# Four instead of six of the first expert's feature blocks in plain fp32

## The chip, the cores and the metric

The kernel runs on one core of a Trainium2 chip. The metric is device time in microseconds of one execution, as the median of several runs. The engines are named as in the profile: PE (TensorE, matmuls), PEld (TensorE's weight loads), DVE (VectorE), ACT (ScalarE), POOL (GpSimd) and SP (SyncE, which here only issues loads).

## The reference

```python
x = retention(q, k, v)                 # 8 batches, 8 heads, 576 positions, 64 wide -> 4608 tokens x 512
g_idx = argmax(x @ w_group)            # 4 groups
e_idx = argmax(x @ w_expert[g_idx])    # 4 experts in the group: 16 experts in all
h  = maximum(x[mine] @ w1[g, e], 0)    # 512 -> 1024, for the tokens of expert (g, e)
ye = h @ w2[g, e]                      # 1024 -> 512
out[mine] = (g_w * e_w)[:, None] * ye  # weights of the two softmaxes
```

Everything is fp32. A token goes through one expert of the sixteen.

## The kernel before

**Stages.** The first stage goes over 36 tiles of 128 tokens: retention, the gates, the choice of an expert, and a place for each token in a table `xs` in device memory, sorted by expert, into which an indirect store on POOL writes the weighted token row (`xnat_store`). The second stage goes over the experts, the fullest first, in steps `p` = 0 to 15, and a last pass for the rest of the first expert. Step 0 takes only the first 256 rows of the first expert and begins while the last tiles of tokens are still being routed.

**A step.** `xload(p)` loads the rows of the step's expert from `xs` into `xb` (four loads on SP). `xturn` turns them to features x tokens (`xTf`, on DVE, in three parts; for step 0 in two). Then come eight blocks `f` of 128 hidden features each: `layer1(p, f)` makes `ph` = w1 block x tokens, and ACT takes the relu of it, `hh`; `layer2(p, f)` adds w2 block x `hh` to the outputs `py`. In program order `layer2` runs one block behind `layer1`. Weights come in pieces of two blocks: piece `pc` holds blocks 2 pc and 2 pc + 1, a w1 part `r1` and a w2 part `r2` of 512 KB each.

**Split and plain.** A value is split in a high part in a shorter format (ACT, `xTh`, `wh`, `hh`) and the remainder (DVE, `xTl`, `wl`, `hl`), and a product is then three matmuls: high x high, high x low, low x high. `xsplit` splits the tokens, `wsplit` a weight part in two halves (ACT then DVE for each), and `layer1` makes `hh` and `hl` from `ph`. A plain block (`whole(p, f)`: step 0 and `f < WHOLE`) needs none of this: one fp32 matmul on `xTf` and the raw weights `r`, and a relu on ACT. The call `split(2 * pc + f % 2 + 3)` in block `f` splits a part that is used some blocks later: in step 0, block `f` splits part `(f + 3) % 2` of piece `(f + 3) // 2`.

**Order.** PE's order is the order of the program, written by hand. Instructions of DVE, ACT, POOL and SP are chained in program order too where they go through `Ordered` (their line is L117 for all of them, the line of that helper). Each engine works off its own list; waits between engines are by semaphores.

**Around the change.** In step 0 `pick(1)` finds the second expert from a count of most of the tokens. `choose`, `places` and `weigh` route the last group of three tiles (names ending in 35 for the routing, tokens in `xt_last`), `tiles_counted` and `count_experts` make the final counts `cnt` and the rows `pad1` that lie behind the second expert's last token, `xpad(1)` stores rows of zeros there, and `xload(1)` loads the second expert's rows. `rank_experts` (rows `key` to `order` on DVE) sorts the experts. Loads of `xs` wait for earlier stores to it; the stores, of different rows each, don't wait for one another (`apart`).

In block `f == WHOLE` of step 0 (`ahead`) two things differ: `layer2` of the block before comes ahead of `layer1`, and two of the three turns of step 1's rows stand between:

```python
            ahead = (p, f) == (0, WHOLE)
            if ahead:
                layer2(*prev)
                for i in range(2):
                    xturn(1, i, 3)
            layer1(p, f)
```

Of the kernel before, what the change touches and what calls it, by code (L numbers as in the profile page):

```python
# [26 lines left out]
CMAX = CAPS[0]  # L27
EARLY = 256
PICK = 26
WHOLE = 6  # L30
RB = 7
LOADS = 7
WARM = 8
# [32 lines left out]
def moe_retention(ctx, tc, qk, kv, wgt, w1, w2, c_f, out):  # L66
# [8 lines left out]
    xs = dp.tile([E * NS, Q * WQ], F32, name="xs")  # L75
# [16 lines left out]
    last = {}  # L92
# [30 lines left out]
    dve, act, pool, sp = [Ordered(e_) for e_ in (nc.vector, nc.scalar, nc.gpsimd, nc.sync)]  # L123

    def apart(key, inst):

        inst = getattr(inst, "ins", inst)
        tc.declare_no_dep(inst, group=key, reason="rows apart")
        tc.add_to_no_dep_group(key, inst)


    ereg = {}
# [25 lines left out]
    def load_piece(i, parts=(0, 1)):  # L158
        if i < len(pieces):
            raws.setdefault(i, []).extend(wload(*pieces[i], part) for part in parts)  # L160
# [5 lines left out]
    def whole(p, f):  # L166

        return p == 0 and f < WHOLE

# [10 lines left out]
    def ttiles(p):  # L180
        return [(r, min(P, CS[p] - r)) for r in range(0, CS[p], P)]

    def ring(name):

        return gp.tile([P, NB * WQ], F32, name=name, tag="ring", bufs=4)

    def nblocks(p):
        return -(-CS[p] // 32)

    def natural(p):  # L190
        return p in (0, E)
# [26 lines left out]
    def expert_of(p):  # L218
        ereg[p] = nc.values_load(
            order[0:1, p : p + 1] if p % E > 1 else eai[p % E][0:1, 0:1],  # L220
            engines=[mybir.EngineType.SP], min_val=0, max_val=E - 1,
        )

    def xload(p):

        if p >= NPASS:
            return
        if p not in ereg:
            expert_of(p)
        r0 = EARLY if p == E else 0  # L230
        nb = nblocks(p)
        mine = xs.rearrange("(e r) c -> e r c", e=E)[bass.ds(ereg[p], 1)]
        xb = ring(f"xb_{p}").rearrange("p (b w) -> p b w", w=WQ)
        for a in range(Q):
            i_ = sp.dma_start(
                xb[32 * a : 32 * a + 32, 0:nb, :],
                mine[:, r0 : r0 + 32 * nb, a * WQ : (a + 1) * WQ].rearrange("o (b t) c -> t (o b) c", t=32),
            )

            tc.add_to_no_dep_group("xs", i_.ins)  # L240
        xg[p] = xb
        if natural(p):
            nt = len(ttiles(p))
            idn = gp.tile([P, 3, 1], F32, name=f"idn_{p}", tag="idn", bufs=2)
            i_ = sp.dma_start(
                idn[:, 0:nt],
                mine[:, r0 : r0 + nt * P, DQ : DQ + 1].rearrange("o (i p) c -> p (o i) c", p=P),
            )
            tc.add_to_no_dep_group("xs", i_.ins)
            idns[p] = idn  # L250

    def xpad(p):

        apart("xs", pool.indirect_dma_start(
            out=xs, out_offset=bass.IndirectOffsetOnAxis(ap={0: pad0, 1: pad1}.get(p, pads[:, p % E : p % E + 1]), axis=0),
            in_=zero, in_offset=None, bounds_check=E * NS - 1, oob_is_err=False,
        ))
# [12 lines left out]
    def xturn(p, part, of):  # L270

        if part == 0:
            xTs[p] = xpair(f"m{p}")
            if p == 0:

                xTf[p] = wp.tile([P, NKC, EARLY], F32, name="xTf_0", tag="wl1", bufs=3)
            else:
                xTf[p] = ring(f"xTf_{p}")[:, 0 : NKC * CMAX].rearrange("p (k c) -> p k c", k=NKC)
        nb = nblocks(p)
        b0, b1 = nb * part // of, nb * (part + 1) // of  # L280
        dve.transpose(
            xTf[p][:, :, 32 * b0 : 32 * b1].rearrange("p k (b t) -> p b k t", t=32),
            xg[p][:, b0:b1, 0:DQ].rearrange("p b (k f) -> p b k f", f=32),
        )
# [64 lines left out]
    rows = {}  # L349
# [51 lines left out]
    def logits(t):  # L401

        plt = ps_sm.tile([P, RG, P], F32, name=f"plt_{t}", tag="sm")
        for i in range(NKC):
            pe.matmul(  # L405
                plt[32 * i : 32 * i + 32], wgp[:, i, :], tiles[t]["xTg"][:, i], start=True, stop=True
            )
        tiles[t]["lt"] = sm.tile([P, RG, P], F32, name=f"lt_{t}", tag="lt")
        act.copy(tiles[t]["lt"], plt)
# [661 lines left out]
    for p in range(E):  # L1071
        for f in range(NFC):
            pc = p * NPIECE + f // 2
            if p == 0:
                new = {2: (4,), 5: (7,)}.get(f, ())
            else:
                new = range(pc + 3, pc + 5) if f % 2 == 0 else ()
            for i in new:
                if i not in raws and (i >= len(pieces) or pieces[i][0] in ereg):
                    load_piece(i)  # L1080
            if (p, f) == (0, 2):
                load_piece(5, (0,))
            if (p, f) == (0, 0):
                prev = (p, f)
                continue
# [7 lines that stand above are left out]
            if (p, f) == (0, 1):  # L1093
                for t in range(NT - RG, NT):
                    xnat_rows(t)
                places_pe(NT - 4)
                places(NT - 4)
                logits(NT - 1)
                xnat(NT - 6)
                pick(1)  # L1100
                expert_of(1)
            if (p, f) == (0, 2):
                xnat(NT - 4)
                places_pe(NT - 1)
                places(NT - 1)
                weigh(NT - 1)
                xnat(NT - 3, ps_sm)
            if (p, f) == (0, 3):
                xnat(NT - 1, ps_sm)
                xload(1)  # L1110
                load_piece(5, (1,))
                load_piece(6)
            if (p, f) == (0, 4):
                for kc in range(NKC):
                    xsplit(0, kc)
            if (p, f) == (0, 6):
                xturn(1, 2, 3)
                for kc in range(NKC):
                    xsplit(1, kc)
            if 2 * pc + f % 2 + 3 >= WHOLE:  # L1120
                split(2 * pc + f % 2 + 3)
            if not ahead:
                layer2(*prev)
            if f == 0:
                for i in range(NKC if p > 1 else 2):
                    yturn(p - 1, i) if p > 1 else finish(0, i)
            if (p, f) == (0, 1):
                gate_pe(NT - 1)
                choose(NT - 1)
                xnat(NT - 5)  # L1130
            if (p, f) == (0, 2):
                tiles_counted()
                count_experts()
                xnat(NT - 2)
            if (p, f) in ((0, 4), (1, 0), (1, 1)):
                next(ranks, None)
            if (p, f) == (0, 6):
                expert_of(2)
            if f == NFC - 3 and p < E - 1:
                width_of(p + 1)  # L1140
            if (p, f) == (1, 1):
                ids(1)
            if p > 1 and f > 0:
                for b in range(2 * (f - 1), 2 * f):
                    if b < nblocks(p - 1):

                        pool.tensor_copy(pace, hts[p, f][0][0:1, 0:1].bitcast(F32))
                    ystore(p - 1, b)
            if (p, f) == (1, 2):
                xpad(2)  # L1150
                sp.dma_start(cf[:, KC_TRI:KC], c_f[:, KC_TRI:KC])
            if (p, f) == (1, 3):
                xload(2)
            if f == 4 and p and p + 2 <= E:
                xpad(p + 2)
            if f == 5 and p:
                xload(p + 2)
            if (p, f) == (2, 3):
                ov = overflow_places(cp)
                ovt = overflow_tables(*ov, mp, phs, cnt, cf, req, ident, ones, pe, dve)  # L1160
            if p in (2, 3):
                next(ovt, None) if (p, f) >= (2, 3) else None
            if f == NFC - 3 and p:
                for i in range(3):
                    xturn(p + 1, i, 3)
            if f == NFC - 2 and p:
                for kc in range(NKC):
                    xsplit(p + 1, kc)
            if f == NFC - 1 and 0 < p < E - 1:
                ids(p + 1)  # L1170
            if (p, f) in ((5, NFC - 1), (10, NFC - 1), (14, NFC - 1), (E - 1, NFC - 2)):

                pool.drain(fusable=False)
            prev = (p, f)
# [297 lines left out]
```

## Time and profile before

| | us |
|---|---|
| median of 3 runs | 589.14 (588.27 to 590.32) |
| the profiled execution | 589.66 |
| its span, first to last instruction | 587.8 |

The profile's page gives the share of the span in which each engine was busy (PE 97%, DVE 72%, ACT 55%, POOL 44%), and the share of each in the chain of work that ended last (PE 89%, DVE 3%, DMA 2%). The timeline lists instructions of an engine in order of time: start and duration in us, engine, line, operation, output<-inputs with buffer numbers left out, sizes, and in brackets the idle time of the engine before it with what ended it. A row of merged instructions has xN. Times in this document are from the start of the span. The first stage reaches to some 152 us, step 0 from 148 to 183 us, steps 1 to 15 to 566 us.

### The profile page before, as it was taken

How to read it: one execution, taken by the hardware profiler on the slowest of the kernel's cores; microseconds unless marked ns; L12 is line 12 of the kernel's file. 1: busy time of each engine (PE TensorE's matmuls, PEld its weight loads, DVE VectorE, ACT ScalarE, POOL GpSimd, SP SyncE). 2: the span in 40 equal slices, each digit the busy share in tenths (PEclk: the TensorE clock that was granted, in tenths of full speed). 3: DMA queues.
4: the chain of work that ended last, by engine and by line, in shares of the span. 5: the costliest groups of instructions: out<-in, count | busy, mean ns of one | idle time of the engine just before them, and what ended most of it. 6: DMA issues, size and time to landing. Idle time of an engine off the chain costs nothing.

```text
span 587.8 us, 16813 instructions
## 1 busy us (share of the span) xinstructions
PE 572.7 (97%) x6045; PEld 535.8 (91%) x6045; DVE 424.7 (72%) x997; ACT 325.3 (55%) x849; POOL 260.8 (44%) x391
## 2 busy tenths in 40 slices
PE   8999899999999999999999999999999999999995
PEld 6888788787769999999999999999999999999994
DVE  4877767768669677966767675867768687687784
ACT  5677787777356445444545444444545455455563
POOL 0022333224332027473636457383654836638454
PEclk9999999999999999999999999999999999999999
DMA  8999899965988961929285656839286594855841
GB/s 325 406 398 343 313 351 341 319 254 156 369 237 329 212 265 59 332 64 325 71 317 138 250 142 255 278 114 335 77 313 176 215 305 118 312 167 218 306 189 38
DMA packets 62410, 143.03 MB, mean 243 GB/s; under 512 B 9425, under 2 KB 30297, under 8 KB 62304
## 3 DMA queue, kind: packets, MB, share of 16 engines
q1 hardware_dynamic: 52944, 121.24, 59.3%
q0 software_dynamic: 9216, 20.28, 9.5%
q8 instruction: 73, 1.20, 0.8%
q14 instruction: 33, 0.27, 0.1%
q10 hardware_dynamic: 144, 0.05, 0.0%
HBM read 121.27 MB, written 24.81 MB: 249 GB/s over the span
## 4 chain that ended last, share of the span: by engine, by line
PE 89%; DVE 3%; issue 2%; DMA 2%; ACT 2%; POOL 1%; SPq 0%; POOLq 0%; ACTq 0%; DVEq 0%
PE ph L593 32%; PE py L995 11%; PE py L997 11%; PE py L996 11%; PE px L790 5%; PE pss L746 4%; PE pxt L363 3%; PE px L808 3%; PE pst L775 2%; PE pss L735 2%; PE plt L405 1%; PE ph L579 1%; DMA xb<-xs 1%; PE py L984 1%; POOL out L117 1%
## 5 line engine op out<-in xcount | busy, mean ns | idle before, releaser
L117 POOL DMA_INDIRECT out<-y,ii x151 | 165.9, 1099 | 64.8 <-issue 31.3
L117 DVE TENSOR_TENSOR wl<-r,wh 128x512 fp32r<-128x512 f32 x260 | 167.8, 687 | 5.9 <-issue 2.4
L117 ACT ACTIVATE hh<-ph 128x256 fp32r<-128x256 f32 (+15 forms) x128 | 53.8, 421 | 202.6 <-PE ph L593 124.4
L117 ACT CAST wh<-r 128x512 fp32r<-128x512 f32 x260 | 147.0, 617 | 0.0
L593 PE MATMUL ph<-xTh_m,wh 128*128 128x324 f32 (+16 forms) x488 | 145.0, 297 | 0.0
L593 PE MATMUL ph<-xTh_m,wl 128*128 128x324 f32 (+16 forms) x488 | 144.3, 296 | 0.0
L593 PE MATMUL ph<-xTl_m,wh 128*128 128x324 f32 (+16 forms) x488 | 144.2, 296 | 0.0
L995 PE MATMUL py<-hh,wh 128*128 128x320 f32 (+19 forms) x480 | 143.2, 298 | 0.8 <-ACT hh L117 0.7
L997 PE MATMUL py<-hl,wh 128*128 128x332 f32 (+14 forms) x480 | 141.8, 295 | 0.0
L996 PE MATMUL py<-hh,wl 128*128 128x332 f32 (+14 forms) x480 | 141.8, 295 | 0.0
L117 DVE SCALAR_TENSOR_TENSOR hl<-ph,hh 128x256 fp32r<-128x256 f32 (+14 forms) x122 | 56.7, 465 | 97.4 <-ACT hh L117 57.8
L593 PEld LDWEIGHTS ph<-xTh_m,wh 128*128 128x128 f32 x488 | 92.1, 189 | 0.4 <-issue 0.2
L593 PEld LDWEIGHTS ph<-xTl_m,wh 128*128 128x128 f32 x488 | 92.1, 189 | 0.4 <-issue 0.2
L593 PEld LDWEIGHTS ph<-xTh_m,wl 128*128 128x128 f32 x488 | 92.2, 189 | 0.0
L995 PEld LDWEIGHTS py<-hh,wh 128*128 128x128 f32 x480 | 90.5, 189 | 1.7 <-ACT hh L117 0.9
L117 POOL COPY pace<-hh 1x1 f32<-1x1 f32 x140 | 33.6, 240 | 129.2 <-ACT hh L117 117.3
L996 PEld LDWEIGHTS py<-hh,wl 128*128 128x128 f32 x480 | 90.7, 189 | 0.0
L997 PEld LDWEIGHTS py<-hl,wh 128*128 128x128 f32 x480 | 90.4, 188 | 0.0
L117 POOL DMA_INDIRECT xs<-xt,sl x33 | 32.8, 993 | 108.2 <-DVE xT L117 40.3
L117 ACT ACTIVATE vs<-b,cf 128x64 f32<-128x64 f32 x288 | 72.4, 336 | 7.0 <-DMA b<-in_kv 5.9
L117 DVE TENSOR_TENSOR sT<-pss,masks 128x512 f32<-128x512 f32 x72 | 46.0, 681 | 13.3 <-PE pss L735 6.9
L790 PE MATMUL px<-sT,vs 128*64 128x128 f32 x576 | 40.5, 283 | 0.7 <-issue 0.6
(194 smaller groups left out, 621.6 us busy)
## 6 DMA issues: line engine op xcount, KB each, us to landing
r<-in_w SPq DMA_DIRECT2D x138, 512.0 KB
a<-in_qk SPq DMA_DIRECT2D x35, 512.0 KB
b<-in_kv SPq DMA_DIRECT2D x35, 512.0 KB
xb<-xs SPq DMA_DIRECT2D x20, 165.0 KB
xb<-xs SPq DMA_DIRECT2D x20, 148.5 KB
out<-y,ii POOLq DMA_INDIRECT x151
xb<-xs SPq DMA_DIRECT2D x12, 181.5 KB
xb<-xs SPq DMA_DIRECT2D x8, 132.0 KB
```

What stands on the lines that cost most here:

```text
L117: i_ = f(*a, **k)
L363: pe.transpose(T["pxt"][:, i, :], T["xT"][:, i, :], ident)
L405: pe.matmul(plt[32 * i : 32 * i + 32], wgp[:, i, :], tiles[t]["xTg"][:, i], start=True, stop=True)
L593: pe.matmul(ph[:, :w], a[:, kc, cs], b[:, kc, :w], start=n == 0, stop=n == 3 * NKC - 1)
L735: pe.matmul(pss[:, o, i * P : i * P + P], T["kT"][r, i, :], T["qT"][r, i, :], start=True, stop=True,)
L746: pe.matmul(pss[k_, o, (i + par) * P + late * D : (i + par + 1) * P], T["kT"][r, i + par, k_], T["qT"][r, i + par, late * D : P], start=Tr ...
L775: pe.matmul(pst[o * D : o * D + D, i, :], T["k"][:, h, :], T["vs"][:, h, :], start=first and i == 0, stop=True, skip_group_check=True,)
L790: pe.matmul(px[g * D : g * D + D, o, s * P : s * P + P], T["vs"][:, 4 * s + 2 * g + o, :], T["sT"][:, o, 2 * s + g, :], start=s == 0, stop ...
L808: pe.matmul(px[g * D : g * D + D, o, s * P + r * w : s * P + r * w + w], st[rows, 2 * s + g, :], T["qT"][rows, 2 * s + g, r * w : r * w + ...
L995: pe.matmul(py[:, :w0], wh[:, f % 2, ds_], hh[:, :w0], start=st_, stop=False)
L996: pe.matmul(py[:, :w], wl[:, f % 2, ds_], hh[:, :w], start=False, stop=False)
L997: pe.matmul(py[:, :w], wh[:, f % 2, ds_], hl[:, :w], start=False, stop=sp_)
```

## The change

Blocks 4 and 5 of step 0 are split products instead of plain ones. `WHOLE` also moves the block with `ahead`, and with it two turns of step 1's rows, from block 6 to block 4; the split of step 0's tokens goes from block 4 to block 2. Piece 2 of the first expert is now split too, its w1 part in block 1 and its w2 part in block 2. A wait is added to the loads of the second expert's rows, for the store of the rows of zeros behind its last token.

```diff
-WHOLE = 6
+WHOLE = 4
...
 def apart(key, inst):
     ...
         tc.add_to_no_dep_group(key, inst)
+        return inst
...
 def xload(p):
     ...
             tc.add_to_no_dep_group("xs", i_.ins)
+            if p == 1:
+                tc.add_manual_dep(
+                    i_.ins, padded[1].name,
+                    mybir.DependencyInfo(mybir.DependencyClass.Sync, mybir.DependencyReason.DATA),
+                    reason="rows behind the last token",
+                )
...
+    padded = {}
+
     def xpad(p):
 
-        apart("xs", pool.indirect_dma_start(
+        padded[p] = apart("xs", pool.indirect_dma_start(
...
-            if (p, f) == (0, 4):
+            if (p, f) == (0, WHOLE - 2):
                 for kc in range(NKC):
                     xsplit(0, kc)
```

The new order is read from the instructions of each engine as built. Names carry the step and block: `hl_0_4` is the low part of block 4 of step 0, `wl1_0_3` the low part of the w2 part of step 0's piece 3 (`wl0` of w1), `xTf_1` the turned rows of step 1; the last number is that of the buffer.

VectorE in step 0 before, from the second part of piece 3 on:

```order
L117 TENSOR_TENSOR wl1_0_3_3352<-r2_0_3_3051,wh1_0_3_3351 128x512 x2
L117 SCALAR_TENSOR_TENSOR key_3359<-cnt_72,cf_64 128x16
L117 SCALAR_TENSOR_TENSOR key_3359<-e0h_68,key_3359 128x16
L117 SCALAR_TENSOR_TENSOR key_3359<-e1h_69,key_3359 128x16
L117 TENSOR_TENSOR kk_3363<-key_3359 128x256
L117 TENSOR_REDUCE rk_3365<-kk_3363 128x16
L117 TENSOR_TENSOR req_75<-rk_3365,cf_64 128x256
L117 TENSOR_TENSOR kk_3363<-req_75,cf_64 128x256
L117 TENSOR_REDUCE order_73<-kk_3363 128x16
L117 TENSOR_TENSOR wl0_1_0_3382<-r1_1_0_3220,wh0_1_0_3381 128x512 x2
L117 STREAM_TRANSPOSE xTf_1_3396<-xb_1_3317 128x4x4x32 x2
L117 SCALAR_TENSOR_TENSOR hl_0_6_3413<-ph_0_6_3399,hh_0_6_3400 128x256
```

The turns come last here but for `hl_0_6`; blocks 4 and 5 have no `hl`.

VectorE now, from the first part of piece 3 on:

```order
L117 TENSOR_TENSOR wl0_0_3_3349<-r1_0_3_3049,wh0_0_3_3348 128x512 x2
L117 STREAM_TRANSPOSE xTf_1_3360<-xb_1_3337 128x4x4x32 x2
L117 SCALAR_TENSOR_TENSOR hl_0_4_3377<-ph_0_4_3363,hh_0_4_3364 128x256
L117 TENSOR_TENSOR wl1_0_3_3381<-r2_0_3_3051,wh1_0_3_3380 128x512 x2
L117 SCALAR_TENSOR_TENSOR key_3386<-cnt_72,cf_64 128x16
L117 SCALAR_TENSOR_TENSOR key_3386<-e0h_68,key_3386 128x16
L117 SCALAR_TENSOR_TENSOR key_3386<-e1h_69,key_3386 128x16
L117 TENSOR_TENSOR kk_3390<-key_3386 128x256
L117 TENSOR_REDUCE rk_3392<-kk_3390 128x16
L117 TENSOR_TENSOR req_75<-rk_3392,cf_64 128x256
L117 TENSOR_TENSOR kk_3390<-req_75,cf_64 128x256
L117 TENSOR_REDUCE order_73<-kk_3390 128x16
```

The two turns of step 1's rows stand ahead of the second part of piece 3 and of the ranking instead of behind them; `hl_0_4` is new and directly behind the turns. The rows that follow are `hl_0_5` (new), `wl0_1_0`, `hl_0_6` and the third turn.

TensorE from layer 1 of block 4 to layer 1 of block 6, before:

```order
L579 MATMUL ph_0_4_3336<-xTf_0_3013,r1_0_2_3007 128x256 x4
L984 MATMUL py_0_0_3187<-r2_0_1_2920,hh_0_3_3302 128x512
L984 MATMUL py_0_1_3188<-r2_0_1_2920,hh_0_3_3302 128x512
L579 MATMUL ph_0_5_3374<-xTf_0_3013,r1_0_2_3007 128x256 x4
L984 MATMUL py_0_0_3187<-r2_0_2_3009,hh_0_4_3337 128x512
L984 MATMUL py_0_1_3188<-r2_0_2_3009,hh_0_4_3337 128x512
L203 TENSOR_LOAD sizes_74
L984 MATMUL py_0_0_3187<-r2_0_2_3009,hh_0_5_3375 128x512
L984 MATMUL py_0_1_3188<-r2_0_2_3009,hh_0_5_3375 128x512
```

Layer 2 of a plain block is one matmul for each of the two token tiles and reads `hh` alone.

TensorE now, layer 2 of block 4 and the beginning of layer 1 of block 6 (lines from here on are numbered nine higher):

```order
L993 MATMUL py_0_0_3193<-wh1_0_2_3288,hh_0_4_3364 128x512
L993 MATMUL py_0_0_3193<-wl1_0_2_3289,hh_0_4_3364 128x512
L993 MATMUL py_0_0_3193<-wh1_0_2_3288,hl_0_4_3377 128x512
L993 MATMUL py_0_1_3194<-wh1_0_2_3288,hh_0_4_3364 128x512
L993 MATMUL py_0_1_3194<-wl1_0_2_3289,hh_0_4_3364 128x512
L993 MATMUL py_0_1_3194<-wh1_0_2_3288,hl_0_4_3377 128x512
L204 TENSOR_LOAD sizes_74
L602 MATMUL ph_0_6_3433<-xTh_m0_3011,wh0_0_3_3348 128x256
```

Ahead of these stand, now, layer 2 of block 2 and of block 3 in a row, and then layer 1 of blocks 4 and 5 (twelve matmuls each). Layer 2 of block 5 now follows layer 1 of block 6.

GpSimd, the last stores of tokens and the store of zeros, before:

```order
L117 IOTA xt_32_3238 128x4x4
L117 DMA xs_63<-xt_32_3238,sl_32_3142 75776x528
L117 DMA xs_63<-xt_last_3129,sl_35_3252 75776x528 x2
L117 DMA xs_63<-zero_83,pad1_80 75776x528
L117 DMA xs_63<-xt_last_3129,sl_35_3252 75776x528
L117 DMA out_0<-y_0_3504,ii_0_3109 4608x512
```

The zeros (`zero_83`) go out between the second and the third tile of the last three.

GpSimd now, the same place:

```order
L117 IOTA xt_32_3244 128x4x4
L117 DMA xs_63<-xt_32_3244,sl_32_3142 75776x528
L117 DMA xs_63<-xt_last_3129,sl_35_3258 75776x528 x3
L117 DMA xs_63<-zero_83,pad1_80 75776x528
L117 DMA out_0<-y_0_3544,ii_0_3109 4608x512 x2
```

The store of zeros stands behind the last token store instead of ahead of it.

## The prediction

> **What bounds the kernel now.** I read the page first, then the waits of TensorE by stretch, then the chain in order of time around step 0, then the timeline of each engine there. The page's first part gives the shares of the span, the waits are those of TensorE from 183 us to the end, and the two last lines are pieces of the chain (start, us, what).
>
> ```profile
> PE 572.7 (97%) x6045; PEld 535.8 (91%) x6045; DVE 424.7 (72%) x997; ACT 325.3 (55%) x849; POOL 260.8 (44%) x391
> ...
> PE py L995 <- ACT hh L117: 0.7, 1, 0.7
> PE py L984 <- ACT hhn L117: 0.2, 1, 0.2
> ...
> 171.17 4.49 DMA xb<-xs
> 175.68 1.30 DVE xTf L117 x2
> ```
>
> TensorE is the bound, and after 183 us it waits 0.9 us in all. So whatever moves its arrival at step 1 moves the end by as much. The chain also shows a second thread just before: the rows of the second expert (`xb`) land and VectorE turns them at 175.68. Both threads meet at the start of step 1, and the change touches both.
>
> The timeline of TensorE in step 0 (start, duration, line, tiles; several rows merged as xN):
>
> ```profile
> 166.24 1.89 PE L579 MATMUL ph<-xTf,r 128*128 128x256 f32 x8
> 167.97 1.88 PE L984 MATMUL py<-r,hh 128*128 128x512 f32 x4
> 169.68 1.89 PE L579 MATMUL ph<-xTf,r 128*128 128x256 f32 x8
> 171.41 3.60 PE L984 MATMUL py<-r,hh 128*128 128x512 f32 x8
> ...
> 176.27 0.28 PE L593 MATMUL ph<-xTh_m,wh 128*128 128x256 f32 x1
> ...
> 177.71 0.39 PE L984 MATMUL py<-wh,hh 128*128 128x512 f32 x1
> ...
> 179.08 0.33 PE L593 MATMUL ph<-xTh_m,wh 128*128 128x356 f32 x1
> ...
> 183.01 0.32 PE L593 MATMUL ph<-xTh_m,wh 128*128 128x356 f32 x1
> ```
>
> 166.24 is layer 1 of block 4, 167.97 layer 2 of block 3, 169.68 layer 1 of block 5, 171.41 layer 2 of blocks 4 and 5; 176.27 and 177.71 are layer 1 of block 7 and layer 2 of block 6, already split; 179.08 and 183.01 are blocks 0 and 1 of step 1.
>
> **Part 1, the matmuls.** Start to start, a plain layer 1 takes 171.41 - 169.68 = 1.73 us, a split one 177.71 - 176.27 = 1.44. A plain layer 2 takes 169.68 - 167.97 = 1.71, a split one 179.08 - 177.71 = 1.37. Two blocks save 2 x (0.29 + 0.34) = 1.26 us of TensorE.
>
> **Part 2, the work added.** VectorE in the same stretch:
>
> ```profile
> 157.13 0.41 DVE L117 TENSOR_REDUCE lg<-pl 128x60 f32<-128x240 f32 x1 [0.66 <-PE pl L418]
> ...
> 162.09 0.17 DVE L117 COPY cnt<-pcn 128x16 f32<-128x16 f32 x1 [0.69 <-PE pcn L913]
> ...
> 163.41 0.16 DVE L117 SCALAR_TENSOR_TENSOR pad<-f,pd_pad 128x1 int32<-128x1 f32 x1
> ...
> 168.87 1.43 DVE L117 TENSOR_TENSOR xTl_m<-xTf,xTh_m 128x256 fp32r<-128x256 f32 x4 [1.64 <-ACT xTh_m L117]
> 170.31 1.29 DVE L117 TENSOR_TENSOR wl<-r,wh 128x512 fp32r<-128x512 f32 x2
> 171.52 0.17 DVE L117 SCALAR_TENSOR_TENSOR key<-cnt,cf 128x16 f32<-128x16 f32 x1
> ...
> 174.31 1.28 DVE L117 TENSOR_TENSOR wl<-r,wh 128x512 fp32r<-128x512 f32 x2
> 175.68 1.30 DVE L117 STREAM_TRANSPOSE xTf<-xb 128x512 f32<-128x512 f32 x2
> 176.94 0.42 DVE L117 SCALAR_TENSOR_TENSOR hl<-ph,hh 128x256 fp32r<-128x256 f32 x1
> 177.29 0.70 DVE L117 STREAM_TRANSPOSE xTf<-xb 128x512 f32<-128x512 f32 x1
> 178.54 1.85 DVE L117 TENSOR_TENSOR xTl_m<-xTf,xTh_m 128x356 fp32r<-128x356 f32 x4 [0.56 <-ACT xTh_m L117]
> ```
>
> A pair of weight subtractions takes 171.52 - 170.31 = 1.21 us. The first pair of the new split stands ahead of `lg`; 0.66 us of it falls into the idle time shown there, so the routing of the last tokens comes about 0.5 us later, and the waits for TensorE that follow (0.69 us ahead of `cnt` is one) give some of it back. I take 0.25; the ends are nothing and 1.2. The third w1 piece must have landed by then. The list of transfers has for 145.3 to 155.6 us (queue, packets, MB, share):
>
> ```profile
> q1 hardware_dynamic: 1005, 2.72, 79.2%
> ```
>
> The four loads that end with this piece are 2.1 MB, and some 0.5 MB of the first expert's rows come ahead of them; so it is just there.
>
> ScalarE, GpSimd and the load queue:
>
> ```profile
> 161.50 0.69 ACT L117 ACTIVATE xt_last<-pxt,wt 128x512 f32<-128x512 f32 x1 [0.94 <-DVE wt L117]
> ...
> 168.44 1.31 ACT L117 CAST xTh_m<-xTf 128x256 fp32r<-128x256 f32 x4
> 169.66 1.14 ACT L117 CAST wh<-r 128x512 fp32r<-128x512 f32 x2
> ...
> 165.20 0.98 POOL L117 DMA_INDIRECT xs<-zero,pad  x1 [0.30 <-issue]
> 166.48 1.01 POOL L117 DMA_INDIRECT xs<-xt_last,sl  x1 [0.30 <-issue]
> ...
> 169.58 1.91 SPq L117 DMA_DIRECT2D xb<-xs  x4
> ```
>
> The token split (ScalarE 169.66 - 168.44 = 1.22, VectorE 1.43) and the second weight pair (about 1.05 on ScalarE) now stand between the `xt_last` of 161.50 and the counting. ScalarE is through at 161.5 + 0.25 + 0.6 + 1.22 + 1.05 = 164.6, VectorE a subtraction later, at 165.3. So `cnt` starts at 165.3 instead of 162.09, and the pad rows, 1.48 us behind it (162.09 to 163.57), are known at 166.8 instead of 163.6. The last two token rows leave ScalarE at 165.2 and 166.1, so the last token store keeps its 166.5. The store of pad rows, formerly ahead of it, is now behind it, one issue of 1.28 us later: 167.8.
>
> The load of `xb` was issued 169.58 - 166.48 = 3.1 us after the last store and had landed 6.1 us after that (175.66 by the chain). It now waits for the pad store: 167.8 + 3.1 = 170.9, landed 177.0. The ends are 176.0, if the pad store, which writes few rows, lands sooner, and 178.0.
>
> **Part 3, the wait that decides.** The two turns of `xb` moved from step 0's block 6 to its block 4. On VectorE they stand ahead of `hl` of block 4, and that row is new work: a plain block needs none. VectorE reaches the turns at about 168.3 and holds there until 177.0, 8.7 us, where before it came at 175.5 and waited 0.2. Queued behind: `hl` of block 4, a weight pair, the ranking, `hl` of block 5, another weight pair, `hl` of block 6. For the first of these TensorE waits.
>
> On TensorE layer 2 of block 3 now stands where layer 1 of block 4 stood, at 166.24, and is reached some 0.4 us late because of the routing, at 166.6. Then 1.71 + 2 x 1.44 bring it to 171.2. Of the six matmuls of layer 2 of block 4, two go without `hl` (0.45); at 171.65 it stops. `hl` is done at 177.0 + (176.94 - 175.68) + 0.35 = 178.6. That is 6.95 us of stall.
>
> Next late is `hl` of block 5: behind `hl` of block 4 stand 1.21 + (174.31 - 171.52 = 2.79) + 0.35, so 182.95. TensorE at full clock is there at 178.6 + 0.92 + 1.44 + 0.45 = 181.4 and waits 1.5 more. From 182.95: 0.92 + 1.44 + 1.37 = 186.7, block 0 of step 1 begins (179.08 before); VectorE's third turn, at 182.95 + 1.21 + 0.35 = 184.5, and the split of step 1's tokens behind it (2.4 us) just keep up. Block 1 follows 1.92 + 1.37 later, 190.0 against 183.01: **+7.0 us at full clock.** All of it passes to the end, since nothing after 183 us holds slack to absorb it.
>
> **The clock behind a stall.** TensorE's last matmuls and the granted clock, by windows (us, five busy columns, clock, DMA), and the same sixteen matmuls near the start:
>
> ```profile
> 5.82 2.08 PE L735 MATMUL pss<-a 64*128 64x128 f32 x16 [1.17 <-DVE gq L117]
> 9.29 2.08 PE L735 MATMUL pss<-a 64*128 64x128 f32 x16 [0.33 <-DVE sT L117]
> 13.83 1.16 PE L735 MATMUL pss<-a 64*128 64x128 f32 x16
> ...
> 581.25 0.40 PE L984 MATMUL py<-wh,hln 128*128 128x512 f32 x1
> ...
> 582.00:586.90 4.90, 0.00 (x0) 0.00 (x0) 0.00 (x0) 0.27 (x1) 0.97 (x1) 1.00 0.09 33
> 587.00:587.80 0.80, 0.00 (x0) 0.00 (x0) 0.00 (x0) 0.00 (x0) 0.00 (x0) 0.50 0.08 20
> ```
>
> Between 5.3 and 6 us after its last matmul TensorE had half its clock; the stall of 6.95 us is longer. At the start the same work took 2.08 us and then 1.16, so half clock lasted somewhere between nothing and 12 us of work there; the stretch without a gap, 9.29 to 13.83, is the nearest to what follows the stall, and I take its 4.5 us. From 178.6 at half clock, the rest of block 4's layer 2 and layer 1 of block 6 take 4.7 instead of 2.36, which hides the second wait of 1.5; block 1 of step 1 then starts at about 190.8: **+7.8 us.** The ends are +7.0 (no half clock) and +11.8 (12 us of it).
>
> [...]
>
> **Sum.** The profiled execution took 589.66 us, span 587.8 plus 1.9 around it; that is 0.5 above the median of 589.14. 589.66 + 7.8 = 597.5, and 0.5 less for the median of runs: **597.0 us**.
>
> **The rivals.**
> - *Stall at full clock*: the clock returns at once or never drops; +7.0, 596.2 us. For it: the margin between 6.95 and 5.3 to 6 us is small. 0.27.
> - *Longer half clock or `xb` at 178*: +9 to +11.8, 598.2 to 601. 0.13.
> - *A stall half as long*: `xb` lands at 173 to 175, since its loads meet no other traffic; +2 to +5, 591.1 to 594.1. Against it: the loads before met little either, their weights were issued behind them. 0.05.
> - *Not slower*: `hl` of block 4 isn't held. That needs `xb` landed by 171.65 - 1.61 = 170.0, before its load is even issued in my count, or turns that don't hold what is behind them; VectorE's rows above start strictly in their order. Then the 1.26 saved less 0.4 late remains, 588.3 us, and 587.9 with nothing late: within 0.3% either way. 0.05, of which 0.01 for something further that brings it below 587.4.
> - My forecast, stall and some 4.5 us of half clock: 0.50.
>
> A difference under 0.3% (1.8 us) can't be told from no change here. Faster 0.01, same 0.04, slower 0.95. The range runs from 593.9, the top of the short stall, to 600.6, most of the long half clock.
>
> **What would show it.** In the profile after: VectorE idle for 8 to 9 us ahead of the first `xTf<-xb` of step 1, released by the DMA; TensorE idle for about 7 us in layer 2 of step 0, put down to `hl`; a granted clock under 1.00 from about 177 us; block 1 of step 1 near 190.8. The forecast is wrong if `xb` lands before 172 or if TensorE shows no stall over 3 us in step 0.

## The result and the profile after

| | us | ratio to before (95%) |
|---|---|---|
| before, median of 6 runs | 588.62 (587.24 to 590.32) | |
| changed, median of 6 runs | 594.92 (594.03 to 596.41) | 1.0133 (1.0104 to 1.0162) |
| changed, the profiled execution (span) | 594.03 (592.2) | |

The change makes the kernel slower by 1.3%. The forecast was 597.0 with a range of 593.9 to 600.6.

The page's lines on busy time and on the granted clock (in tenths, 40 slices):

```profile
PE 568.0 (96%) x6057; PEld 534.6 (90%) x6057; DVE 427.2 (72%) x1003; ACT 328.1 (55%) x853; POOL 259.9 (44%) x391
...
PEclk9999999999989999999999999999999999999999
```

TensorE's waits from 146 us to the end (in total, times, longest):

```profile
PE py L993 <- DVE hl L117: 7.3, 1, 7.3
PE ph L602 <- issue: 0.9, 1, 0.9
PE py L1004 <- ACT hh L117: 0.6, 1, 0.6
PE pxt L372 <- ACT xt L117: 0.2, 1, 0.2
```

One slice has lost clock, and one new wait of 7.3 us stands in layer 2 of step 0, for an `hl`. TensorE is busy 4.7 us less than before, but that is not the work that the change saves: in the first stage it is busy 5.1 us less (135.1 against 140.2), and from there to block 1 of step 1 it is busy 0.8 us more (35.8 against 34.9). The timeline of TensorE after the change:

```profile
143.89 1.99 PE L588 MATMUL ph<-xTf,r 128*128 128x256 f32 x8 [0.67 <-DVE xTf L117]
...
167.49 0.40 PE L993 MATMUL py<-wl,hh 128*128 128x512 f32 x1
175.18 0.79 PE L993 MATMUL py<-wh,hl 128*128 128x512 f32 x1 [7.28 <-DVE hl L117]
...
177.05 0.41 PE L602 MATMUL ph<-xTh_m,wh 128*128 128x256 f32 x1
177.26 0.41 PE L602 MATMUL ph<-xTl_m,wh 128*128 128x256 f32 x1
...
187.16 0.32 PE L602 MATMUL ph<-xTh_m,wh 128*128 128x356 f32 x1
```

143.89 is the first plain matmul of step 0, 175.18 the third matmul of block 4's layer 2, 177.05 layer 1 of block 6, 187.16 block 1 of step 1. VectorE, and the stores and loads of the second expert's rows (POOL, SP's queue):

```profile
158.96 1.43 DVE L117 TENSOR_TENSOR xTl_m<-xTf,xTh_m 128x256 fp32r<-128x256 f32 x4 [1.11 <-ACT xTh_m L117]
160.40 1.29 DVE L117 TENSOR_TENSOR wl<-r,wh 128x512 fp32r<-128x512 f32 x2
161.61 0.17 DVE L117 COPY cnt<-pcn 128x16 f32<-128x16 f32 x1
...
173.51 1.30 DVE L117 STREAM_TRANSPOSE xTf<-xb 128x512 f32<-128x512 f32 x2 [9.16 <-DMA xb<-xs]
174.74 0.39 DVE L117 SCALAR_TENSOR_TENSOR hl<-ph,hh 128x256 fp32r<-128x256 f32 x1
175.04 1.27 DVE L117 TENSOR_TENSOR wl<-r,wh 128x512 fp32r<-128x512 f32 x2
...
179.03 0.42 DVE L117 SCALAR_TENSOR_TENSOR hl<-ph,hh 128x256 fp32r<-128x256 f32 x1
...
180.90 0.70 DVE L117 STREAM_TRANSPOSE xTf<-xb 128x512 f32<-128x512 f32 x1
...
164.31 0.98 POOL L117 DMA_INDIRECT xs<-zero,pad  x1 [0.30 <-issue]
...
167.15 1.90 SPq L117 DMA_DIRECT2D xb<-xs  x4
```

VectorE stands still for 9.16 us ahead of the two turns, and everything that was behind them in the program comes behind them in time.

**The measure used below.** The first stage, which the change does not touch, ends at chance times: the first plain matmul of step 0 stands at 147.88 us in the profile of before and at 143.57 in a second one of the same kernel, and between 143.05 and 148.55 over all 14 profiles of this study. These 5.5 us are nearly as much as the change costs, and they are in every run's time. So I count from the first plain matmul of step 0 to the start of block 1 of step 1: before 183.01 - 147.88 = **35.13 us**, after 187.16 - 143.89 = **43.27 us, 8.14 more**. What follows block 1 is alike: 404.8 us to the end before, 405.0 after, and 404.2 and 404.4 in a second profile of each. In this pair of profiles the span grew by only 4.4, because the first stage happened to be 4.0 shorter.

### The profile page after: what moved, and what is told of

Its sections match the earlier page's. It is cut to its first block, busy times and chain, and to the rows that moved or that the text cites. A ratio compares the mean times of both kernels' runs of the same rounds, so it can differ in the third digit from the quotient of the medians.

```text
span 592.2 us, 16849 instructions
## 1 busy us (share of the span) xinstructions
PE 568.0 (96%) x6057; PEld 534.6 (90%) x6057; DVE 427.2 (72%) x1003; ACT 328.1 (55%) x853; POOL 259.9 (44%) x391
## 4 chain that ended last, share of the span: by engine, by line
PE 84%; DVE 5%; DMA 4%; ACT 2%; issue 2%; POOL 1%; SPq 1%; POOLq 0%; ACTq 0%; DVEq 0%
PE ph L602 33%; PE py L1004 11%; PE py L1005 11%; PE py L1006 11%; PE px L799 4%; PE pss L755 3%; DMA r<-in_w 2%; PE px L817 2%; PE pxt L372 2%; PE pst L784 2%; PE plt L414 1%; PE py L993 1%; DVE sT L117 1%; DMA b<-in_kv 1%; ACT vs L117 1%
## 5 line engine op out<-in xcount | busy, mean ns | idle before, releaser
L117 DVE TENSOR_TENSOR wl<-r,wh 128x512 fp32r<-128x512 f32 x264 | 170.5, 687 | 3.6
L117 ACT CAST wh<-r 128x512 fp32r<-128x512 f32 x264 | 149.3, 617 | 0.1
L602 PE MATMUL ph<-xTh_m,wl 128*128 128x324 f32 (+16 forms) x496 | 147.1, 297 | 0.9 <-issue 0.9
L602 PE MATMUL ph<-xTh_m,wh 128*128 128x324 f32 (+16 forms) x496 | 147.8, 298 | 0.0
L602 PE MATMUL ph<-xTl_m,wh 128*128 128x324 f32 (+16 forms) x496 | 147.0, 296 | 0.0
L602 PEld LDWEIGHTS ph<-xTh_m,wh 128*128 128x128 f32 x496 | 94.1, 190 | 1.7 <-issue 1.3
L602 PEld LDWEIGHTS ph<-xTl_m,wh 128*128 128x128 f32 x496 | 94.1, 190 | 0.5 <-DVE wl L117 0.2
L602 PEld LDWEIGHTS ph<-xTh_m,wl 128*128 128x128 f32 x496 | 94.2, 190 | 0.0
L117 POOL COPY pace<-hh 1x1 f32<-1x1 f32 x140 | 31.7, 226 | 130.4 <-ACT hh L117 120.5
```

The source lines that it names most:

```text
L117: i_ = f(*a, **k)
L602: pe.matmul(ph[:, :w], a[:, kc, cs], b[:, kc, :w], start=n == 0, stop=n == 3 * NKC - 1)
```

## The experiments

All figures from traces are counted from the first plain matmul of step 0. "Turns" is where VectorE begins the first turn of the second expert's rows, "tail" the difference from there to block 1.

| kernel | turns | block 1 | tail | time against before (95%) |
|---|---|---|---|---|
| before | 27.80 | 35.13 | 7.33 | |
| before, again | 27.77 | 35.14 | 7.37 | |
| changed | 29.62 | 43.27 | 13.65 | 1.0133 (1.0104 to 1.0162) |
| changed, again | 30.63 | 44.15 | 13.52 | 1.0186 (1.0135 to 1.0238) |
| turns back at block 6 | 30.66 | 37.91 | 7.25 | 1.0058 (1.0030 to 1.0085) |
| counting early again | 29.31 | 42.81 | 13.50 | 1.0151 (1.0105 to 1.0196) |
| both | 28.56 | 35.81 | 7.25 | 1.0015 (0.9989 to 1.0041) |
| before, turns at block 4 | 28.39 | 42.98 | 14.59 | one run |
| TensorE kept busy | 29.55 | 42.69 | 13.14 | 1.0160 (1.0095 to 1.0225) |
| changed, without two `hl` | 30.33 | 43.78 | 13.45 | one run |
| before, less TensorE work | 28.08 | 35.33 | 7.25 | one run |
| three turns behind block 6's layer 1 | 28.90 | 35.83 | 6.93 | 1.0022 (0.9997 to 1.0048) |
| and the ranking late | 28.27 | 35.20 | 6.93 | 1.0006 (0.9978 to 1.0034) |
| ranking and a weight split placed anew | 28.49 | 34.78 | 6.29 | 0.9986 (0.9956 to 1.0017) |

Block 1 is the sum of two things that the experiments move one at a time: when the rows are turned, and the tail behind.

**The two kernels again, unedited.**

> The changed kernel once more, unaltered. The step from the first plain matmul of step 0 to block 1 of step 1 was 35.1 us before and 43.3 us after, 8.1 longer, yet the medians of runs differ by 6.3. If the missing 1.8 us is chance in the first stage (3.98 us shorter in the one profile of after), the runs here differ by 7 to 9 us, ratio 1.012 to 1.015. If the first stage really is shorter with the change, they differ by 5.5 to 6.8, ratio 1.009 to 1.0115. The step itself should be 42.5 to 44 us in either case, with 7 us of stall and 6.8 us of half clock.

> The kernel before, for a second profile. If the length of the first stage varies by chance, the first plain matmul of step 0 starts anywhere from 143 to 149 us (147.9 in the first profile), with the full clock granted at another time than 13.5 us; the step stays 35.1 within 0.3 us, and from block 1 of step 1 to the end 404.8 within 0.5. If it is tied to the kernel, it is 147 to 148.5 again.

The step before is 35.13 and 35.14 us; after, 43.27 and 44.15. The second value differs by its turns (30.63), not by its tail, and lies a little above the 44 that I gave. The time in this set is 1.9% over before, some 11 us, above both of my ranges, where the first set had 1.3%. So the times alone place the loss only between 6 and 11 us; the step says 8 to 9. The first plain matmul of the kernel before stands at 143.57 this time, so its place varies within one kernel.

**The two turns back at block 6, the rest of the change kept.**

```diff
+            if (p, f) == (0, 6):
                 for i in range(2):
                     xturn(1, i, 3)
```

> The change as it is, but the two turns of step 1's rows go back to block 6. Theory queue (VectorE held at the turns until the rows land, and what stands behind them sets step 1): the stall in layer 2 of block 4 is gone, the turns are held at block 6 until the rows land 1.3 us later than before, hl of block 6 comes some 1 us late; the step is 35.2 to 36.5 us and the time 0 to 1 us over before, ratio 1.000 to 1.002. Theory work (the added splits on ScalarE and VectorE and the later counting are the loss, wherever the turns stand): the step stays above 40 us, ratio above 1.008.

The step is 37.91: of the 8.14 us 5.4 are gone, and against the second profile of the changed kernel, whose turns begin at the same time (30.63), 6.2. TensorE's waits from 146 to 195 us, and from the timeline the turns:

```profile
PE py L993 <- DVE hl L117: 2.0, 3, 1.0
PE pxt L372 <- ACT xt L117: 0.9, 1, 0.9
```

```profile
177.70 1.30 DVE L117 STREAM_TRANSPOSE xTf<-xb 128x512 f32<-128x512 f32 x2 [1.32 <-DMA xb<-xs]
```

No wait is over 1.05 us, and the matmuls of layer 1 of blocks 6 and 7 take 0.28 us each, against 0.41 at half clock in the changed kernel (177.05). The tail is that of before. What is left, 2.8 us, is the later landing (177.70 - 147.04 = 30.66), larger than I had expected; with it the step and the ratio (1.0058) lie above the ranges of the theory that held.

**The token split and a weight split back behind the counting, the turns still early.**

```diff
-            if (p, f) == (0, WHOLE - 2):
-                for kc in range(NKC):
-                    xsplit(0, kc)
...
-            if 2 * pc + f % 2 + 3 >= WHOLE:
+            if 2 * pc + f % 2 + 3 >= WHOLE and (p, f) != (0, 2):
...
                 xnat(NT - 2)
+                for kc in range(NKC):
+                    xsplit(0, kc)
+                split(5)
```

> The change as it is, but in block 2 the split of the tokens and of the w2 part of piece 2 come behind the counting and the last token rows, so that the zeros behind the second expert's last token are stored ahead of the last token store, as before. Theory queue: the rows land 1.3 us earlier than with the change, the stall in layer 2 of block 4 falls from 7.3 to about 6 us, the step from 43.3 to about 42; 1.0 to 1.6 us faster than the change. Rival (the landing doesn't set the stall, the length of VectorE's list does): no difference over 0.3 us in the step. Clock: with a stall of 6 us half clock may or may not come; without it the step is 41.

`cnt` is back at 14.78 (before 14.21, after 161.61 - 143.89 = 17.72), but the load of the rows is issued only 0.8 us earlier than in the changed kernel (22.49 against 23.26), since the last token row now stood behind a split on ScalarE (its store begins at 19.54, before at 18.60), and the rows' transfer took 6.8 us instead of 6.4. The step falls to 42.81, not to the 42 that I had expected. The two profiles of the changed kernel lie 0.9 apart, so how much this part is worth while the turns stand early isn't settled; it is small against that of the turns.

**Both.**

> The changed kernel with the two turns back at block 6 and the token split and the second half of the third weight split back behind the counting and the last token rows. Measure: the step from its first plain matmul to block 1 of step one, 35.13 us before, 43.27 and 44.15 after, 37.91 with the turns alone moved back, 42.81 with the counting alone moved back. Theory (two causes that add: the turns that wait on VectorE ahead of other work, and a later landing of the rows): the rows land as in the kernel with the counting alone moved back, 29.3 us after the first plain matmul instead of 30.7, and the step falls by that much below 37.91, to 36.3 to 36.8; time +1 us on before. Rival (the landing does not matter, what is left is the work behind the turns at block 6): step stays at 37.7 to 38.0.

35.81: turns 28.56, tail 7.25, and the time can't be told from that of before. Without the early turns the tail is 7.25 to 7.37 in five profiles, whenever the turns begin. The turns come 2.1 us sooner than with the early turns alone undone, since the loads are issued at 22.31 instead of 23.90. They no longer show the landing: VectorE begins them right behind a weight pair (from 173.91, the turns at 175.11, no idle time between), so the rows had landed by then, at most 6.25 us after the issue. The step is below the 36.3 to 36.8 that I had expected, since the rows landed sooner than the 29.3 that I had taken.

**The kernel before with nothing but the turns moved.**

```diff
             if ahead:
                 layer2(*prev)
+            if (p, f) == (0, 4):
                 for i in range(2):
                     xturn(1, i, 3)
```

> The kernel before, with six plain blocks, and only the two turns moved from block 6 to block 4. Theory (the turns alone hold VectorE): counting and the pad store as before, the rows issued at 21.5 to 21.7 and landed at 27.8 us after the first plain matmul, VectorE idle ahead of the turns from about 18.5 to 27.8, and the low halves of the tokens (ready at 21.0 to 22.4 in the kernel before) behind them, so that layer one of block 6 starts at 31 us or later instead of 26.6; the step is 38.5 to 41 us against 35.13. Rival (the turns cost only together with the split of four blocks): the step stays within 1 us of 35.13.

42.98: the two turns alone, in a kernel with six plain blocks, cost 7.85 us, more than I had expected and nearly what the whole change costs. TensorE's two waits:

```profile
176.34 0.38 PE L593 MATMUL ph<-xTl_m,wh 128*128 128x256 f32 x1 [2.82 <-DVE xTl_m L117]
...
182.88 0.50 PE L984 MATMUL py<-wh,hl 128*128 128x512 f32 x1 [1.56 <-DVE hl L117]
```

They are 4.4 us together, so they don't make up the loss. Behind the turns stand here the low halves of step 0's tokens, two weight pairs, the ranking and `hl` of block 6; from the end of the two turns to the third turn that is 182.74 - 175.91 = 6.83 us against 0.35 before. Half clock comes on top: from the third turn to block 1 it is 6.53 us against 5.72. Windows of this kernel (five busy columns PE, PEld, DVE, ACT, POOL, then granted clock, DMA, GB/s):

```profile
177.50:180.90 3.40, 3.40 (x17) 3.36 (x16) 3.16 (x10) 0.38 (x1) 0.00 (x0) 0.50 0.69 276
180.90:184.30 3.40, 1.84 (x7) 0.86 (x5) 2.85 (x6) 0.82 (x3) 0.00 (x0) 1.00 0.28 90
184.30:187.70 3.40, 3.28 (x11) 3.12 (x11) 3.40 (x8) 3.19 (x8) 0.00 (x0) 0.50 0.95 313
```

Each of the two waits is followed by one stretch of 3.4 us at half clock, the second of them in block 0 of step 1.

**TensorE kept busy through its wait.**

```diff
+            if (p, f) == (0, 5):   # ahead of layer 2 of block 4
+                pf = ps_sm.tile([P, 4, P], F32, name="pf", tag="sm")
+                for i in range(28):
+                    pe.matmul(pf, ones, ..., start=True, stop=True)
```

> The changed kernel with 28 extra matmuls of the ones tile into a spare PSUM tile ahead of layer two of block 4, where TensorE otherwise stands still for 7.3 us; nothing of the output hangs on them. Theory (half clock costs little, since it runs beside VectorE's own late work): no granted clock of 0.5 in this stage, layer one of block 6 at 0.12 us a matmul instead of 0.21, and then a wait on the hl of block 5 that was hidden before; the step is 42.2 to 43.1 us against 43.27 and 44.15. Rival (half clock costs the 4.5 us times one half that it lasts after the stall, 2.3 us): the step falls to 41 to 41.9. If the extra matmuls take longer than the stall, the step grows by what they stand over the rows' landing, which the trace shows.

Windows from 166 us on (columns as above), and then TensorE's wait for `hl` from 143 to 200 us:

```profile
166.00:180.00 14.00, 12.80 (x73) 8.46 (x72) 4.72 (x12) 2.82 (x6) 1.41 (x2) 1.00 0.81 243
180.00:190.00 10.00, 8.76 (x50) 7.60 (x49) 9.34 (x21) 6.34 (x15) 0.00 (x0) 1.00 0.77 274
```

```profile
PE py L993 <- DVE hl L117: 2.4, 2, 1.2
```

The clock stays at 1.00, and the wait for `hl` of block 5 that half clock had hidden comes out (1.24 us). The tail falls from 13.65 to 13.14: half clock costs about 0.5 us, not the 2.3 that 4.5 us of it would cost with nothing beside it. From the third turn to block 1 it is 6.26 us in the changed kernel, 5.76 here and 5.72 before. The time can't show a difference of this size.

The chain of waits of the changed kernel from `hl` of block 4 on (start, us, what):

```profile
174.81 0.32 DVE hl L117
175.18 2.07 PE py L993 x4
177.25 2.55 PE ph L602 x12
179.80 1.39 PE py L993 x6
```

From here to block 1 it holds TensorE's matmuls alone. So in the changed kernel itself TensorE's work at half clock sets block 1, with VectorE's queue half a microsecond behind it; at full clock, in the kernel of this experiment, TensorE waits for `hl` of block 5, which stands in that queue.

**The changed kernel without the two `hl`.**

```diff
+        if (p, f) in ((0, 4), (0, 5)):
+            act.activation(hh[:, :C], ph[:, :C], AF.Relu)
+            hts[p, f] = (hh, None)
+            return
...
+                ab = ab[:2] if hl is None else ab
```

> The changed kernel, leaving out the low half of the activations of blocks 4 and 5 and its product with the high half of the weights, so that TensorE has nothing to wait for behind the two early turns until layer one of block 6 has run. Theory (VectorE's work queued behind the turns sets the step, and the 7.3 us wait is only where it shows): TensorE's wait moves to layer two of block 6 and to step one's tokens, and the step falls only by the two hl and the two products left out and some half clock, to 41.3 to 42.8 us against 43.27 and 44.15. Rival (the stall itself is the cost): the step falls by 6 us or more, to 36 to 38.

TensorE's waits from 143 to 200 us:

```profile
PE py L998 <- DVE hl L117: 4.1, 1, 4.1
PE py L998 <- DVE wl L117: 3.7, 1, 3.7
```

The wait of 7.3 us in layer 2 of block 4 is gone, two others of 7.8 us in all have come, and the step is 43.78, between the two profiles of the changed kernel. My own figure (41.3 to 42.8) was low by 1 us, since the rows landed late here (30.33) and half clock lasted 10.2 us, into block 0 of step 1 (6.72 us from the third turn to block 1, against 6.26 in the changed kernel); the rival, that the wait itself is the cost (36 to 38), is out.

**The kernel before with 1.7 us less for TensorE.**

```diff
             for i, (r0, n) in enumerate(ttiles(p)):
+                if i and f in (4, 5):
+                    continue
```

> The kernel before, leaving out the second token tile of layer two in blocks 4 and 5 (its products are missing from the sum), so that TensorE has 1.7 us less to do ahead of block 6 and nothing else is changed. It asks what the 1.26 us that the split of two blocks saves on TensorE could bring in the kernel before. Theory (VectorE's chain from the landed rows, turns, low halves, weight split and hl of block 7, sets block 1 of step one already before): layer one of block 6 starts 1.7 us earlier (24.9 instead of 26.6 us after the first plain matmul), the turns stay at 27.7 to 27.9, and the step is 34.7 to 35.13 us. Rival (TensorE's work sets it): the step is 33.4 to 33.8.

Layer 1 of block 6 starts at 24.85 instead of 26.56, and block 1 of step 1 at 35.33 instead of 35.13. TensorE arrives sooner and then waits 1.0 us for `hl` of block 6 (the rows landed 0.3 later). So in the kernel before TensorE was not what held block 1 up, although it waits almost nowhere. The chain of waits of before shows what did (start, us, what):

```profile
175.68 1.30 DVE xTf L117 x2
176.99 0.38 DVE hl L117
177.37 0.63 DVE xTf L117
...
178.41 1.27 ACT xTh_m L117 x3
179.68 1.04 ACT wh L117 x2
180.72 0.28 ACT hh L117
181.00 0.52 ACT wh L117
181.52 0.42 DVE hl L117
181.94 0.04 issue
181.98 1.19 PE py L984 x4
```

From the turns it runs through the third turn, the token split, a weight split and `hl` of block 7, 6.3 us in which TensorE's own work only runs beside. The prediction showed the first line of this chain and read it as a second thread; it was the one that decided.

**Four plain blocks in an order that VectorE can serve.** First all three turns behind layer 1 of block 6, the second half of the third weight split behind the last token row, the token split behind the counting; then, also, the first half there and the ranking in block 7.

> The changed kernel with all three turns of step one behind layer one of block 6, so also behind its hl, the token split back behind the counting in block 2, and the second half of the third weight split in block 3, behind the last token rows on ScalarE. Theory (order on VectorE and ScalarE alone costs the time): the transfer of the rows is issued 21.5 to 22.0 us after the first plain matmul (21.5 to 21.7 before, 22.5 with the counting alone moved back, where the last token row stands 1.0 us behind a weight split), the rows land at 27.8 to 28.5, no stall over 1 us is left on TensorE, the step is 34.4 to 35.8 us against 35.13, and the time within 0.7 us of before. Rival (the four blocks' split itself is too much work for VectorE or ScalarE wherever it stands): the step stays above 36.5 and the time over 1 us above before.

> The kernel with all three turns behind layer one of block 6, with two more moves: both halves of the third weight split behind the last token row (block 3), and the ranking of the experts with the read of the third expert's number that follows it from blocks 4 and 6 to block 7, behind the turns. Theory (in the changed kernel with its order put right, VectorE's own queue to the turned rows sets block 1 of step one, and the rows' landing is its floor): the ranking no longer stands ahead of hl of block 5 and of the turns, the 0.7 us wait in layer two of block 5 goes, VectorE waits for the rows ahead of the turns, which come at 27.7 to 28.5 us after the first plain matmul instead of 28.9; the step is 34.3 to 35.3 us against 35.83 with the three turns behind block 6 and 35.13 before; the time within 1 us of before. Rival (something else than VectorE's queue holds TensorE there): the step stays at 35.6 to 36.2.

The first gives 35.83, with the turns at 28.90 and the time 1.3 us over before, each a little beyond what I had expected; the time can't be told from before. Its turns have no idle time ahead of them: VectorE was still at its queue when the rows came. With the ranking out of that queue VectorE waits 1.42 us for the rows, the turns begin at 28.27 and the step is 35.20, within what I had expected but no gain; and the ranking, now in step 1, holds the next `hh` up, so that block 2 of step 1 stands at 40.27 against 38.99 before.

**The ranking between `hl` of blocks 5 and 6, and a weight split behind `hl` of block 7.**

```diff
...
+            if (p, f) == (0, 7):
+                split(9)
-            if 2 * pc + f % 2 + 3 >= WHOLE:
+            if 2 * pc + f % 2 + 3 >= WHOLE and (p, f) not in ((0, 1), (0, 2), (0, 6)):
...
-            if (p, f) in ((0, 4), (1, 0), (1, 1)):
+            if (p, f) in ((0, 5), (1, 0), (1, 1)):
                 next(ranks, None)
...
```

> A candidate from the readings so far, four plain blocks: the kernel with the late ranking, but the ranking between hl of block 5 and hl of block 6, where VectorE was idle for 2.4 us, and the second half of step one's first weight split behind hl of block 7 instead of ahead of it. Theory (VectorE's queue between the landed rows and hl of block 7 sets block 1 of step one, so taking a weight split of 1.2 us out of it sets TensorE's saving free): the turns start 28.1 to 28.7 us after the first plain matmul, layer two of block 7 doesn't wait, the step is 34.2 to 34.8 us against 35.13 before and 35.20 with the late ranking, and block 2 of step one stands at 37.9 to 38.7 us against 38.99 and 40.27; that is 0.3 to 1.0 us less than before, under what the times can tell. Rival (the landing of the rows alone sets it, whatever follows): the step stays at 35.0 to 35.4.

The chain of waits of this kernel, where that of before had 178.41 to 181.94:

```profile
177.13 1.81 DVE xTf L117 x3
...
179.48 0.54 DVE xTl_m L117
...
180.07 2.04 PE ph L602 x11
182.10 1.39 PE py L993 x6
```

The weight split is out of the chain, TensorE follows the split tokens directly, and the tail is 6.29: block 1 at 34.78, block 2 at 187.22 - 148.55 = 38.67, 0.3 us less than before in both. The time is 587.05 us against 588.0, a ratio of 0.9986 (0.9956 to 1.0017): not to be told from before. So of the 1.26 us that four plain blocks save on TensorE no more than some 0.3 arrive in this one profile. Whether they come from that saving or from the weight split that stands elsewhere isn't shown: the kernel before was not run with that split moved.

## Why the prediction was right, and where it was off

**The account of the 8.14 us.** Later turns: 29.62 - 27.80 = 1.82. VectorE's queue: from the end of the two turns to the third turn it needs 177.29 - 176.94 = 0.35 before, for one `hl`, and 180.90 - 174.74 = 6.16 after, for three `hl`, two weight pairs and the ranking; that is 5.81 more. It is the same 5.81 by which the tail of the kernel with TensorE kept busy exceeds that of before (13.14 - 7.33). Half clock: 13.65 - 13.14 = 0.51. Sum 8.14. These are differences between single profiles; the turns of the changed kernel alone vary by 1.0 from one to the other, the tails by 0.1.

- *The mechanism* held: VectorE idle for 9.16 us (8 to 9 said, 8.7 worked out), TensorE for 7.28 (6.95 said), released by `hl`, block 1 later by 8.14 (7.8 said), and all of it passed to the end.
- *The saving of 1.26 us* was sized right as far as the trace shows it (a split layer 1 takes 167.27 - 165.83 = 1.44 us there too), and TensorE came to its stop 24.0 us after the first plain matmul (175.18 - 7.28 - 143.89), 23.8 as worked out. But it was no gain to be had: with 1.7 us less to do, TensorE's arrival at block 1 didn't move. "Whatever moves its arrival at step 1 moves the end" holds for delays only.
- *The landing* is the term that was mis-sized: turns 1.32 us later were said (177.0 - 175.68), 1.82 and 2.86 were measured. Of the first 0.5 us excess, 0.24 lies ahead of the loads' issue and 0.26 in the transfer, 6.36 us instead of 6.1. Ahead of the issue, the step that failed is "the last token store keeps its 166.5": it begins at 19.14 instead of 18.60. GpSimd waits 1.51 us for ScalarE ahead of the store before it, and the stores follow one another every 1.28 us, so the store of zeros begins at 20.42 instead of the 19.9 that was worked out; the loads follow it by 2.8 us instead of 3.1. The counting itself was not the limit: `cnt` came 3.51 us later instead of 3.21, but the rows for the zeros were known 1.2 us before their store began. In the second profile the transfer took 6.80. On the time of the profile before, 30.63 would be 178.5, beyond the upper end of 178.0 that I gave.
- *The second wait* of 1.5 us for `hl` of block 5 did not show in the changed kernel, since half clock hid it, as worked out; with TensorE kept busy it was 1.24 (1.5 said).
- *Half clock* was granted for as long as assumed, 4.5 us behind the stall:

```profile
167.70:175.20 7.50, 0.22 (x2) 0.03 (x1) 1.69 (x4) 1.24 (x3) 0.00 (x0) 0.84 1.01 259
175.20:179.70 4.50, 4.50 (x17) 4.12 (x18) 4.26 (x12) 0.00 (x0) 0.00 (x0) 0.50 0.83 330
179.70:187.20 7.50, 7.50 (x44) 6.73 (x44) 6.94 (x16) 5.55 (x13) 0.00 (x0) 1.00 0.81 270
```

In these windows of the changed kernel (columns as above) the clock is 0.84 on the mean while TensorE stands, so half for the last 2.4 us of that, and 0.50 until 179.7. I had priced it at 0.8 us; it cost 0.5, since VectorE's queue stands only that far behind TensorE. That the 4.5 us came out to the tenth is luck: they were taken from the start of the kernel before, where the same matmuls took 2.08 and later 1.16 us, but the granted clock in the profile of before is 1.00 all through that stretch, so it isn't shown that half clock was what made them slow, nor that the full clock came at 13.5 us. By the same working the end for 12 us of half clock comes to +11.5, not +11.8. In the kernel before with the early turns the clock was 0.50 also behind 3.4 us in which TensorE was busy for 1.84 (180.90 to 184.30).

- *Which wait decides.* I called TensorE's wait for the turns "the wait that decides". Taking it away leaves the step at 43.78 (the kernel without the two `hl`): the 7.3 us are where the loss shows, and the work queued on VectorE behind the turns keeps it there when they are gone. My sum came out since I had followed that queue step by step.
- *The forecast time* is 2.1 us above the median, and that it is so near is in part luck: the second set of runs gave 1.9% instead of 1.3%. Between profiles of one kernel the first stage alone varies by more, so the time says little on the terms; the step length does.

Not settled: why the first stage ends up to 5.5 us apart in different executions, and why the transfer of the rows, from the first load's issue to the turns, takes from 6.1 to 7.0 us in the profiles where VectorE waits for it (6.4 and 6.8 in two of the same kernel).

## What to carry to other kernels

The two turns that waited 9.16 us for a transfer held up everything behind them on VectorE: what that cost was the work behind them that could have been done meanwhile, here 5.8 us of VectorE, and not the 7.3 us of waiting that TensorE showed. So ask of an instruction that waits what stands behind it. When a part of the order is tied to a constant, look at what else moves with it; here the turns, moved along with `WHOLE`, cost 7.85 us by themselves, six times the 1.26 us that the change of blocks saves on TensorE. And an engine at 97% with no waits is not thereby the one that sets a stage's length: follow the chain to the stage's end, or shorten the engine's work and see whether the end moves.

## What the runs showed of the hardware

The granted clock was half for 3.4 us twice in the kernel before with the early turns (above), for 6.8 us in the changed kernel (from 172.8 to 179.7), and for 10.2 us in the kernel without the two `hl`, whose windows are:

```profile
177.60:187.80 10.20, 5.62 (x15) 4.73 (x16) 9.41 (x22) 4.00 (x9) 0.00 (x0) 0.50 0.79 282
187.80:190.00 2.20, 2.20 (x12) 1.94 (x12) 1.99 (x5) 1.57 (x4) 0.00 (x0) 0.99 0.87 336
```

There TensorE worked for only 0.8 us between two waits of 3.7 and 4.1 us, and the clock came back only 4.8 us behind the end of the second (182.97 to 187.8). In the kernel before with the early turns the clock was half behind waits of 2.8 and 1.6 us (0.50 from 177.5 and from 184.3). Behind the wait of 1.05 us (turns back at block 6) the matmuls of step 1's block 0 took 0.32 to 0.33 us from the third on, against 0.50 at half clock in the kernel without the two `hl`; around the waits of 1.2 us (TensorE kept busy) the granted clock was 1.00. With 28 matmuls of 128x512 that nothing used, 6.2 us, in the wait of the changed kernel it was 1.00 from 166 to 190 us.
